# A delta-rule attention and cosine-gated feed-forward kernel: letting the build-time instruction order count TensorE's slow lengths behind pauses

## The chip, the cores and the metric

The kernel runs on one core of one Trainium2 chip. The core has five instruction queues that run side by side: TensorE (PE, matrix products), VectorE (DVE), ScalarE (ACT), GpSimd (POOL) and SyncE (SP, which here only issues transfers). Each works its instructions off in the order of the program, and waits where an instruction needs something that another queue or a transfer has yet to deliver. The metric is the device time of one execution in microseconds, median of several runs. Before the change it is 701.46 us (three runs, 700.74 to 701.78).

## The reference

The inputs are q, k, v of shape (4, 8, 768, 48), beta of shape (4, 8, 768), and two weight matrices, w_in (384, 2048) and w_out (2048, 384), all float32.

```python
# attention: delta rule, one state of 48x48 per batch and head
k_n = k / (np.linalg.norm(k, axis=-1, keepdims=True) + 1e-06)
state = np.zeros((B, H, D, D), dtype=np.float32)
for t in range(S):
    kt, vt, bt = (k_n[:, :, t], v[:, :, t], beta[:, :, t, None])
    y[:, :, t] = np.einsum('bhd,bhde->bhe', q[:, :, t], state)
    v_old = np.einsum('bhde,bhd->bhe', state, kt)
    state = state + bt[:, :, :, None] * np.einsum('bhd,bhe->bhde', kt, vt - v_old)
# bridge: (B, H, S, D) -> (B*S, H*D), then the feed-forward block
x = y.transpose(0, 2, 1, 3).reshape(B * S, H * D)      # 3072 x 384
h = x @ w_in                                           # 3072 x 2048
g = h * np.cos(h)
return g @ w_out                                       # 3072 x 384
```

The kernel works the attention off in 24 units of 32 time steps. In a unit it forms the products of keys and queries among themselves ("gram"), inverts a triangular 32x32 matrix per batch and head ("inverse", for two units at once), and then passes the state on: state product, right side, solve, update, within. The result of a unit is transposed ("features") and becomes 128 rows of x. Two units are a pair, for which the feed-forward block is computed: eight hidden products, the gate on ACT and DVE, and the output products. The units form one chain through the state; the feed-forward products fill TensorE in between.

## The kernel before

Every piece of work is a task with an engine, a cost in us, what it depends on, and a deadline. While the program is built, the class `Order` plays these tasks through with the costs given, and writes each engine's instructions in the order that results. Nothing of it runs on the chip: it settles the order in each queue and nothing else.

```python
class Order:
    WINDOW = 133.06
    LAG = {"PE": 0.2, "DVE": 0.15, "ACT": 0.15, "POOL": 0.2, "SP": 2.0}
    IN_FLIGHT = 8
    STICK = 4.36
    CHANGE = 0.15
    SMALL = ("gram", "state", "solve", "update", "within")
    BLOCK, PHASE, AHEAD, FETCH = 256, 63, 38, 3.5
    ...
    def stall(self, key, now, commit):
        # PE's instructions are counted; a block of 256 of them that is
        # fetched too late adds a wait to the task's cost
    ...
    def run(self, wrote):
        ...
                # the task with the earliest deadline that is ready and has its buffers
                if engine == "PE":
                    if (key[0] in self.SMALL) != small:
                        small = not small
                        cost += self.CHANGE
                    cost += self.stall(key, now, True)
                running[key] = item[0]
                ...
                emit()
                ...
                free[engine] = start + cost
```

The tasks that matter here, cut to their core:

```python
    # constants that the deadlines are formed with
    W_IN, W_OUT, LOADS = 62.2, 33.46, -16.83
    START = 67.36
    FIRST, STEP = 3.98, 5.5
    BASE = [START + (8 * FIRST + (p - 1) * 8 * STEP if p else 0) for p in range(NU // 2 + 2)]

    def weights(t):                 # t 0..11: pieces of w_in, 12..27: of w_out
        c = 1.0 if t < 12 else 0.8
        add(("weights", t), "SP", 0.45, lambda: narrow_load(t), ...,
            makes=[("g", ("pairs", t))], moves=1.5 * c, due=LOADS + 2 * t)
        add(("split", t), "ACT", 1.4 * c, lambda: narrow_split(t), [("weights", t)])
        add(("shift", t), "DVE", 1.4 * c, lambda: narrow_shift(t), [("split", t)])
        add(("add", t), "POOL", 1.45 * c, lambda: narrow_add(t), [("shift", t)],
            uses=[("pairs", t)], due=W_IN + 2 * t if t < 12 else W_OUT + 2 * (t - 12))

    # a unit n of the attention (m = n // 2)
        add(("turn", n), "PE", 0.9, ...)        # transposes of k and q into PSUM (p_t)
        add(("turn_out", n), "ACT", 1.25, ...)  # two copies to SBUF (kq_t)
        add(("gram", n), "PE", 0.75, ...)       # p_g
        ...
        add(("state", n), "PE", 1.3 if n else 0.0, ...)   # p_kq <- st, kq_t
        add(("right", n), "DVE", 0.58 if n else 0.0, ...) # rhs
        add(("solve", n), "PE", 0.75, lambda: solve(n), [("right", n), ("get", n)], ...)  # p_u
        add(("solve_out", n), "DVE", 1.0, ...)            # u
        add(("update", n), "PE", 0.75, ...)               # p_s; bank "two", as p_t and p_g
        add(("update_out", n), "DVE", 1.0, ...)           # st
        add(("within", n), "PE", 0.75, ...)               # p_kq <- u, tt
        add(("within_out", n), "ACT", 0.52, ...)          # y
        add(("features", n), "PE", 0.35, ...)             # p_z
        add(("features_out", n), "ACT", 0.52, ...)        # x_ffn

    # the feed-forward block of pair p; hidden(0, f) needs 3 (f // 2 % 4 + 1) pieces of w_in
            add(("hidden", *key), "PE", 2.62, lambda f=f: hidden(p, f), deps,
                makes=[("h", ("h", *key))], uses=[("x", p)],
                due=BASE[p] + f // 2 * (STEP if p else FIRST))
            add(("turns", *key), "ACT", 0.65, ...)
            add(("rest", *key), "DVE", 0.73, ...)         # r
            add(("cos", *key), "ACT", 1.45, ...)
            add(("gate", *key), "DVE", 0.73, ...)         # g_ffn
    # the first pair's output products: part k needs 4 (k + 1) pieces of w_out
```

The transfers are issued by SyncE in the written order: `load` (k, q or v of a unit, four transfers each), `narrow_load` (a piece of weights), `put` and `get` (the inverse to device memory, z_dr, and back, zt), `gram_put` and `gram_get` (g_dr and gb). The last pair's seven output products already alternate between two PSUM banks, and its first half of rows is already stored in two pieces.

Of the kernel before, what the change touches and what calls it, by code (L numbers as in the profile page):

```python
# [46 lines left out]
class Order:  # L47
# [9 lines left out]
    WINDOW = 133.06  # L57
    LAG = {"PE": 0.2, "DVE": 0.15, "ACT": 0.15, "POOL": 0.2, "SP": 2.0}
    IN_FLIGHT = 8
    STICK = 4.36  # L60
    CHANGE = 0.15
    SMALL = ("gram", "state", "solve", "update", "within")
# [8 lines left out]
    def __init__(self, bufs, free):  # L71
        self.bufs, self.free = bufs, free
        self.tasks, self.users, self.tiles = {}, {}, {}
        self.written, self.rest, self.there = 0, 0.0, {}

    def add(
# [35 lines left out]
    def run(self, wrote):  # L112
# [26 lines left out]
        count, now = len(self.tasks), 0.0  # L139
        log = []  # L140
        while events:
            now, _, key, done = heapq.heappop(events)
            if key is not None:
# [6 lines left out]
                engine, moves = self.tasks[key][0], self.tasks[key][7]  # L150
# [19 lines left out]
            for engine, heap in ready.items():  # L170
# [6 lines left out]
                if engine == "PE":  # L177
                    if (item[2][0] in self.SMALL) != small:
                        item = min(
                            (  # L180
                                x for x in able
                                if x[0] <= item[0] + self.STICK
                                and (x[2][0] in self.SMALL) == small
# [11 lines left out]
                _, cost, _, emit, _, makes, _, moves = self.tasks[key]  # L195
                if engine == "PE":
                    if (key[0] in self.SMALL) != small:
                        small = not small
                        cost += self.CHANGE
                    cost += self.stall(key, now, True)  # L200
                running[key] = item[0]
                for tag, _ in makes:
                    live[tag] += 1
# [4 lines left out]
                if moves:  # L208
                    flights = sorted(f for f in flights if f > now)
                    if len(flights) >= self.IN_FLIGHT:  # L210
                        start = flights[-self.IN_FLIGHT]
                free[engine] = start + cost
# [14 lines left out]
def kernel(  # L227
# [696 lines left out]
    )  # L924
    add = order.add
    VECTOR = {0: "one"}
    W_IN, W_OUT, LOADS = 62.2, 33.46, -16.83
    PLAIN = range(1)
    outs_done = [None]
    START = 67.36  # L930
    FIRST, STEP = 3.98, 5.5
    BASE = [START + (8 * FIRST + (p - 1) * 8 * STEP if p else 0) for p in range(NU // 2 + 2)]

# [311 lines left out]
```

## Time and profile before

| | before |
|---|---|
| time, median of 3 runs | 701.46 us |
| span of the profiled execution | 699.6 us |
| granted TensorE clock, mean | 0.997 |
| TensorE busy | 639.3 us, 91% |
| VectorE busy | 402.9 us, 58% |
| ScalarE busy | 283.2 us, 40% |
| GpSimd busy | 342.5 us, 49% |
| transfers | 49.27 MB, mean 70 GB/s |

The profile is of one execution. A line of the timeline gives the start and the length in us, the engine, the line of the kernel, the operation with the names of the tiles written and read, how many instructions are merged, and in brackets the idle time before it and what ended it. "issue" is time in which the engine waited for nothing that the profile shows. A table by stages gives each engine's busy time and number of instructions in a stretch, then the granted TensorE clock, the share of time in which the transfer engines were busy, and the rate. Names: p_t transposes, p_g gram, p_kq state product and within, p_u solve, p_s update, p_z features, p_h hidden products, p_out and p_o output products; pairs are pieces of the weights as they come from memory.

### The profile page before, as it was taken

How to read it: one execution, taken by the hardware profiler on the slowest of the kernel's cores; microseconds unless marked ns; L12 is line 12 of the kernel's file. 1: busy time of each engine (PE TensorE's matmuls, PEld its weight loads, DVE VectorE, ACT ScalarE, POOL GpSimd, SP SyncE). 2: the span in 40 equal slices, each digit the busy share in tenths (PEclk: the TensorE clock that was granted, in tenths of full speed). 3: DMA queues.
4: the chain of work that ended last, by engine and by line, in shares of the span. 5: the costliest groups of instructions: out<-in, count | busy, mean ns of one | idle time of the engine just before them, and what ended most of it. 6: DMA issues, size and time to landing. Idle time of an engine off the chain costs nothing.

```text
span 699.6 us, 25291 instructions
## 1 busy us (share of the span) xinstructions
PE 639.3 (91%) x11096; PEld 568.9 (81%) x11096; DVE 402.9 (58%) x804; ACT 283.2 (40%) x482; POOL 342.5 (49%) x738
## 2 busy tenths in 40 slices
PE   3305799999999999999999999999999999999997
PEld 2205697777898988998998988998998988988997
DVE  4895778876655545556556555556456455444542
ACT  3424467652443542532533532532532532433430
POOL 5469678878508607708607707708508508500000
PEclk9999999999999999999999999999999999999999
DMA  9888656562323133133133133132122120110000
GB/s 174 195 173 181 131 144 162 131 121 38 63 54 72 28 73 72 27 74 70 30 72 72 29 70 72 30 73 48 22 57 49 22 58 26 22 22 14 1 23 22
DMA packets 162833, 49.27 MB, mean 70 GB/s; under 512 B 154212, under 2 KB 157428, under 8 KB 162724
## 3 DMA queue, kind: packets, MB, share of 16 engines
q1 hardware_dynamic: 161252, 46.82, 32.6%
q8 instruction: 87, 1.43, 0.9%
q0 software_dynamic: 384, 0.64, 0.4%
q10 hardware_dynamic: 1088, 0.20, 0.1%
q14 instruction: 22, 0.18, 0.1%
HBM read 36.62 MB, written 11.01 MB: 68 GB/s over the span
## 4 chain that ended last, share of the span: by engine, by line
PE 86%; DMA 5%; DVE 4%; issue 1%; ACT 1%; SPq 1%; ACTq 0%; POOL 0%; DVEq 0%
PE p_h L745 32%; PE p_out L850 29%; PE p_kq L625 4%; PE p_h L728 4%; PE p_s L673 3%; PE p_kq L690 3%; PE p_out L792 3%; PE p_u L652 3%; PE p_g L514 2%; PE p_t L496 2%; PE p_o L850 1%; SPq L330 1%; DVE p_i L590 1%; DVE part_v L583 1%; DMA kp<-in_k_dram 1%
## 5 line engine op out<-in xcount | busy, mean ns | idle before, releaser
L745 PE MATMUL p_h<-x_ffn,w_in 128*128 128x256 f32 x1056 | 241.7, 381 | 1.3 <-DVE g_ffn L782 1.3
L583 POOL TENSOR_TENSOR part<-z,gb 128x126 f32<-128x126 f32 (+22 forms) x341 | 131.2, 385 | 218.4 <-DMA gb<-g_dr 167.0
L745 PEld LDWEIGHTS p_h<-x_ffn,w_in 128*128 128x128 f32 x1056 | 197.1, 190 | 26.8 <-PE p_kq L625 1.0
L590 POOL TENSOR_TENSOR z<-z,part 128x126 f32<-128x126 f32 (+22 forms) x341 | 137.1, 402 | 26.7
L762 DVE SCALAR_TENSOR_TENSOR r<-p_h,turns 128x512 f32<-128x512 f32 x96 | 66.1, 689 | 114.9 <-ACT turns L758 113.7
L850 PE MATMUL p_out<-w_out,g_ffn 128*128 128x192 f32 x672 | 126.0, 333 | 0.8
L758 ACT ACTIVATE turns<-p_h 128x512 int32<-128x512 f32 x96 | 57.1, 594 | 167.6 <-PE p_h L745 154.2
L850 PEld LDWEIGHTS p_out<-w_out,g_ffn 128*128 128x128 f32 x672 | 108.7, 190 | 6.2 <-ACT o L887 3.0
L782 DVE TENSOR_TENSOR g_ffn<-r,p_h 128x512 f32<-128x512 f32 x96 | 65.5, 683 | 53.0 <-ACT r L770 52.7
L850 PE MATMUL p_out<-w_sum,g_ffn 128*128 128x192 f32 x496 | 89.7, 329 | 0.2 <-DVE o L900 0.2
L866 DVE TENSOR_TENSOR g_ffn<-g_ffn 128x256 f32<-128x256 f32 x176 | 79.2, 471 | 15.0 <-PE p_out L850 13.0
L769 ACT ACTIVATE r<-r 128x512 f32<-128x512 f32 x96 | 60.7, 632 | 62.0 <-DVE r L762 61.9
L850 PEld LDWEIGHTS p_out<-w_sum,g_ffn 128*128 128x128 f32 x496 | 81.7, 190 | 2.3 <-DVE o L900 0.4
L770 ACT ACTIVATE r<-r,halfpi 128x512 f32<-128x512 f32 x96 | 69.3, 722 | 3.1
L496 PE MATMUL p_t<-consts,kp 128*128 128x128 f32 x96 | 16.8, 305 | 41.2 <-DMA vp<-in_v_dram 29.6
L900 DVE SCALAR_TENSOR_TENSOR o<-p_out,o 128x192 f32<-128x192 f32 x74 | 25.4, 356 | 48.5 <-PE p_out L850 48.2
L496 PEld LDWEIGHTS p_t<-consts,kp 128*128 128x128 f32 x96 | 13.0, 157 | 43.8 <-issue 38.1
L701 ACT COPY y<-p_kq 128x384 f32<-128x384 f32 x24 | 11.5, 479 | 69.5 <-PE p_kq L690 69.5
L455 POOL TENSOR_TENSOR knrm<-ksum,halves 128x16 f32<-128x16 f32 (+1 forms) x14 | 36.5, 2613 | 5.9 <-DVE ksum L443 3.3
L625 PEld LDWEIGHTS p_kq<-st,kq_t 48*32 48x32 f32 x2944 | 29.4, 107 | 7.1 <-issue 7.0
L625 PE MATMUL p_kq<-st,kq_t 48*32 48x48 f32 x2944 | 32.8, 216 | 1.6 <-issue 1.6
L502 ACT COPY kq_t<-p_t 128x512 f32<-128x512 f32 x48 | 25.7, 588 | 15.9 <-PE p_t L496 15.9
(73 smaller groups left out, 619.8 us busy)
## 6 DMA issues: line engine op xcount, KB each, us to landing
pairs<-in_moe_w_in_dram SPq DMA_DIRECT2D x12, 512.0 KB
gb<-g_dr SPq DMA_DIRECT2D x24, 256.0 KB
pairs<-in_moe_w_out_dram SPq DMA_DIRECT2D x16, 384.0 KB
vp<-in_v_dram SPq DMA_DIRECT2D x96, 48.0 KB
kp<-in_k_dram SPq DMA_DIRECT2D x92, 48.0 KB
qp<-in_q_dram SPq DMA_DIRECT2D x92, 48.0 KB
out_dram<-o SPq DMA_DIRECT2D x23, 192.0 KB
g_dr<-g SPq DMA_DIRECT2D x24, 128.0 KB
```

The costliest lines, as they stand in the source:

```text
L496: nc.tensor.transpose(p_t[:, a, j], src[:, 2 * j : 2 * j + 2], ident)
L583: eng.tensor_tensor(out=part, in0=z[:, 0:rows, j, None].to_broadcast(shape), in1=a[:, j, None, j + 1 :].to_broadcast(shape), op=ALU.mult,)
L590: eng.tensor_tensor(out=behind, in0=behind, in1=part, op=ALU.subtract)
L625: nc.tensor.matmul(p_kq[quarter(b), par, a, j], kq_t[rows48(par), a, j, quarter(b)], st[rows48(par), b // 2, j, b % 2], start=(j == 0 and ...
L745: nc.tensor.matmul(p_h[:, i], w_in[:, t, (f + i) * 128 : (f + i + 1) * 128], xts[p][:, t], start=(t == 0), stop=(t == KT - 1),)
L758: nc.scalar.activation(turns[p, f], p_hs[p, f], AF.Copy, scale=TURN)
L762: nc.vector.scalar_tensor_tensor(out=r, in0=p_hs[p, f], scalar=TURN, in1=turns.pop((p, f)), op0=ALU.mult, op1=ALU.subtract,)
L769: nc.scalar.activation(r, r, AF.Abs)
L770: nc.scalar.activation(r, r, AF.Sin, bias=halfpi, scale=-2.0 * math.pi)
L782: nc.vector.tensor_tensor(out=out, in0=rests.pop((p, f)), in1=p_hs.pop((p, f)), op=ALU.mult,)
L850: nc.tensor.matmul(p_o, left(p, e // 2, a)[:, e % 2], right(e, b), start=(e == 0), stop=(e == FT // 2 - 1), skip_group_check=True,)
L866: nc.vector.tensor_tensor(out=left(p, k, to), in0=left(p, k, one), in1=left(p, k, two), op=op)
```

## The change

The build-time order now holds that TensorE is slow behind pauses. It keeps the moment at which TensorE's latest stretch of work began. A gap of more than 0.6 us starts a new stretch, a gap of more than 2.0 us makes the engine cold, 5.0 us of a stretch make it warm again, and the cost of a task on the cold engine counts twice. With it go three constants of the deadlines: those for w_out's addition and for the loads of weights lie later, by 10.3 and 3 us, and so do those for the feed-forward products, by 2.64 us. The kernel's arithmetic and its instructions are the same; what the change is for is an order of them that suits the engine's real lengths at the start.

```diff
@@ class Order
     IN_FLIGHT = 8
+    WARMING = 5.0
     STICK = 4.36
@@ __init__
         self.tasks, self.users, self.tiles = {}, {}, {}
+        self.since, self.last, self.cold = 0.0, 0.0, True
         self.written, self.rest, self.there = 0, 0.0, {}
@@ run
                     cost += self.stall(key, now, True)
+                if engine == "PE" and cost:
+
+                    if now - self.last > 0.6:
+                        self.since = now
+                    if now - self.last > 2.0:
+                        self.cold = True
+                    if now - self.since > self.WARMING:
+                        self.cold = False
+                    cost *= 2.0 if self.cold else 1.0
+                    self.last = now + cost
                 running[key] = item[0]
@@ tile_deltanet__then__act_gcu_kernel
-    W_IN, W_OUT, LOADS = 62.2, 33.46, -16.83
+    W_IN, W_OUT, LOADS = 62.2, 43.76, -13.83
     PLAIN = range(1)
     outs_done = [None]
-    START = 67.36
+    START = 70
```

## The prediction

> **What bounds the kernel now.** I read the slices of the page first, then the busy times by stage, then the waits of TensorE (PE), then the engines' lines in order of time around each wait.
>
> The slices: 40 of 17.5 us each, in tenths busy; PEclk is the granted clock.
> ```profile
> PE   3305799999999999999999999999999999999997
> PEclk9999999999999999999999999999999999999999
> ```
> PE is full from the sixth slice on, and a program of fixed matmuls can't be made shorter there. Only the first five slices and the last are open.
>
> The same by stage (us; busy time of each engine and count of instructions, then clock, DMA share, GB/s):
> ```profile
> 0.00:55.15 55.15, 12.41 (x288) 10.13 (x289) 39.80 (x123) 19.37 (x34) 30.75 (x52) 1.00 0.86 176
> 55.15:115.00 59.85, 50.06 (x1349) 45.74 (x1350) 41.73 (x68) 33.40 (x61) 47.48 (x76) 0.97 0.70 168
> 115.00:200.00 85.00, 83.56 (x1362) 67.21 (x1365) 61.25 (x111) 42.69 (x75) 59.41 (x111) 1.00 0.41 82
> 200.00:694.90 494.90, 493.28 (x8122) 445.78 (x8108) 259.80 (x502) 187.79 (x313) 204.88 (x501) 1.00 0.23 45
> 694.90:699.60 4.70, 0.00 (x0) 0.00 (x0) 0.36 (x1) 0.00 (x0) 0.00 (x0) 0.97 0.17 58
> ```
> PE idles 42.7 us before 55.15 (loads, then the first inverse on VectorE, DVE, from 29.4 to 47.5), 9.8 us in 55 to 115, 1.4 in 115 to 200, 1.6 in the next 495, 4.7 behind the last matmul. So what a new order can win after 55 us is under 13 us of idle time, plus matmuls slowed by the cold clock.
>
> PE's waits from 55 to 200 us (us in total, times, longest):
> ```profile
> PE p_u L652 <- issue: 1.8, 1, 1.8
> PE p_h L728 <- issue: 1.7, 1, 1.7
> PE p_s L673 <- ACT kq_t L502: 1.6, 1, 1.6
> PE p_kq L625 <- issue: 1.6, 1, 1.6
> PE p_s L673 <- DVE u L660: 1.4, 1, 1.4
> PE p_h L745 <- DVE g_ffn L782: 1.3, 2, 0.9
> PE p_h L728 <- DVE r L762: 0.7, 1, 0.7
> ```
> They are many and short, each with another cause. The third is an update (L673) placed right behind a transpose whose result ScalarE (ACT) must still copy out of the same PSUM bank. Two "issue" waits fall where the build-time order's own bookkeeping puts a fetch of PE instructions behind many short matmuls (a state product is 128 of them in 1.4 us).
>
> PE in order of time, the cold clock (start, us, instructions):
> ```profile
> 71.13 4.18 PE L728 MATMUL p_h<-x_ffn,w_in 128*128 128x128 f32 x21 [1.67 <-issue]
> 77.20 2.94 PE L728 MATMUL p_h<-x_ffn,w_in 128*128 128x128 f32 x24
> 88.04 1.25 PE L625 MATMUL p_kq<-st,kq_t 48*32 48x48 f32 x89 [1.56 <-issue]
> 89.22 4.14 PE L728 MATMUL p_h<-x_ffn,w_in 128*128 128x128 f32 x24
> ```
> The same 24 matmuls take 2.94 us or 4.14 us. PE warms by 75.2, and is slow once more from 88 to 93.
>
> [...] the relapse at 88 follows pauses of 1.65, 0.26 and 1.56 us only. The change's rule (cold behind a pause over 2.0 us) wouldn't see this relapse, but would see the one after the long wait. The slow copy is 1.4 times as long here, not 2.
> [...] k, q and v come in rows of 192 B; the page counts 154212 of 162833 packets under 512 B, and the DMA share is 0.86 in the first stage at 176 GB/s. So the order of DMA issues early on matters.
> [...] the weights' shift on DVE (L417) takes 0.68 us at 78.1 and 1.58 us at 86.2, where POOL works too.
>
> **The change part by part.** No instruction is added or removed: PE has the same 5680 matmuls as the program counts them, and its last 495 of 602 groups stand in the same order, as do the last 60 rows of the other queues. PE goes over from small to large matmuls and back 160 times before, 158 after. The constants are only deadlines of the build-time order. So the gain is the difference in the moment at which PE reaches the common order, near 160 us; behind it I expect nothing.
>
> Up to the first state product PE's order is equal. Two things come earlier or later before it. The SyncE queue now:
> ```profile
> 48.17 0.39 SPq L599 DMA_DIRECT2D z_dr<-z  x1
> 48.61 4.88 SPq L330 DMA_DIRECT2D vp<-in_v_dram  x4
> 53.53 0.45 SPq L403 DMA_DIRECT2D pairs<-in_moe_w_in_dram  x1
> 54.08 4.81 SPq L608 DMA_DIRECT2D zt<-z_dr  x8
> ```
> Behind the store of the inverse come one v load, one piece of weights, then the inverse's reload (zt), for which the first solve waits at 58.93. After: the weights, a whole k load, the v load, then zt. Four more issues at 0.48 us (v's 1.9 us per four elsewhere) are **+1.9 us** for the first solve. Behind it, now, DVE does u only at 61.23, 0.3 us after the solve, for a weights shift; after, that shift stands before, so **-0.3**. But ACT's copy of y then stands behind the split of w_in's next to last piece, and x_ffn behind a square that needs a k load: I allow **+0.6**. The first hidden product so starts 2.2 us later; its fetch wait (1.67) stays.
>
> Then the order differs. Now: hidden, solve, gram, hidden, transpose, update, within, gram, features, state, hidden. After: hidden twice, gram, solve, transpose, hidden, update, within, features, hidden, gram, one output product, hidden twice, state. In this:
> - a hidden product lies between transpose and update: **-1.65**, ACT's two copies (1.07) hide under its 2.9 us;
> - gram no longer follows the state's sum directly: **-0.26**;
> - state comes behind six hidden products instead of two, so its instructions are fetched under long matmuls: **-1.56**;
> - without these pauses, no relapse of the clock: 4.14 - 2.94 = 1.2, and 0.3 on the 89 matmuls (0.96 at the warm 1.38 per 128): **-1.5**;
> - the third hidden product needs nine pieces of w_in, which POOL adds behind the second inverse (end 77.0). POOL now waits 4.35 us in its queue:
> ```profile
> 82.59 1.02 POOL L426 TENSOR_TENSOR w_out<-w_out,pairs 128x384 uint32<-128x384 uint32 x1 [4.35 <-DVE w_out L422]
> 83.56 3.79 POOL L426 TENSOR_TENSOR w_in<-w_in,pairs 128x512 uint32<-128x512 uint32 x3
> ```
> After, w_out's first pieces are issued by SyncE before the stores of the second inverse and fourth gram, not behind them, so this wait should vanish: one w_out, one w_in, one w_out, two w_in are 1.0 + 1.3 + 1.0 + 2.6 = 5.9 us, until 82.9. PE arrives at about 82.1 (76.3 end of the first, + 2.9 + 0.8 + 0.9 + 1.2): **+0.8**.
> Sum: +1.9 - 0.3 + 0.6 - 1.65 - 0.26 - 1.56 - 1.5 + 0.8 = **-2.0 us**. In 100 to 160 the waits of 0.7 (r) and 1.3 (g_ffn) stem from DVE queued behind w_out pieces; after, w_out is nearly done earlier, three pieces before the third inverse. But the output products want them earlier too: the third product at about 118 against 133 now, with POOL's twelfth piece at 115 to 117. Half of the 2.0 us saved: **-1.0**. That is 3.0 less in all; rounding for what I can't see in the queues, I take 2.7: **698.8 us**.
>
> **Rivals.** *The start decides against it.* If zt, y and x_ffn together cost 4 to 5 us instead of 2.2, the gain is eaten: 701 to 702. For it: DMA is the busy part there (share 0.86), and ACT takes pieces in order. Against it: a k load moves out of the stretch behind.
> *The output products wait for w_out.* POOL interleaves these adds with the third inverse; if gb comes 3 us late, each of two products waits some 2 us: 702 to 704. For it: PE now has that gram 7 us later. Against: SyncE now blocks gb until 92.4 though it is ready earlier.
> *The new order avoids nearly all waits.* All idle time of 62 to 130 (about 7 us) and the relapse gone, and zt not late: 695. For it: this is what the cold clock in the build-time order is for. Against: the order's idea of DMA times was not changed.
> *Nothing moves*, as PE is full from 90 us on: within 1 us of 701.5. Against it: idle time before 90 shifts everything behind.
>
> **Range and chances.** The terms sized from single rows add up to -5.0 and +3.3; the start is uncertain by some 2 us and the output products by 2. Range 695.4 to 702.4. A 2% step is 14 us, more than all idle time behind 55 us, so faster by over 2% 0.02, within 0.96, slower 0.02.
>
> **What would show it.** In the changed kernel: the first solve at about 60.5 instead of 58.9; no wait of update on kq_t; no issue wait at a state product near 86; hidden products of 2.9 us throughout from 77 on; a wait of under 1 us of the third hidden product on POOL; busy time of PE some 1.5 to 2 us less; all behind 200 us shifted as a block. I'm wrong if PE's waits on w_in or w_out pieces exceed 3 us, if the first solve moves by over 3 us, or if the stretch behind 200 us changes length.

## The result

| | before | after |
|---|---|---|
| time, median of 4 runs each, same comparison | 701.28 us (700.74 to 701.78) | 707.68 us (706.85 to 708.43) |
| ratio to before | | 1.0091, 95% interval 1.0074 to 1.0109 |
| span of the profiled execution | 699.6 us | 705.1 us |
| TensorE busy | 639.3 us | 639.7 us |

The prediction was 698.8 us, with a range up to 702.4. The kernel became 6.4 us slower instead of 2.7 us faster, and the time lies outside the range.

The profile after, first its slices (tenths busy, then the granted clock):

```profile
PE   3306887999999999999999999999999999999997
...
PEclk9755899999999999999999999999999999999999
```

The sixth and the seventh slice (88 to 123 us) have fallen from 9 tenths to 8 and 7, the fifth has risen from 7 to 8; from the eighth on PE is full as before. The stages that answer to those shown of before (us; busy time and instructions of PE, PE's weight loads, DVE, ACT, POOL; clock, DMA share, GB/s):

```profile
0.00:55.15 55.15, 12.52 (x291) 10.49 (x292) 40.10 (x123) 19.90 (x36) 30.52 (x52) 0.75 0.88 188
55.15:115.00 59.85, 45.16 (x999) 40.02 (x1000) 40.22 (x66) 31.19 (x59) 46.53 (x71) 0.80 0.73 171
115.00:200.00 85.00, 82.77 (x1575) 66.80 (x1565) 57.55 (x106) 39.73 (x71) 59.49 (x116) 1.00 0.35 68
200.00:600.00 400.00, 399.15 (x7203) 358.60 (x7199) 217.50 (x414) 158.54 (x265) 195.57 (x475) 1.00 0.27 53
```

PE has 45.16 us of work in the second stage where it had 50.06, and 82.77 in the third where it had 83.56. Behind 200 us it is as full as it was. So the loss is made between 55 and about 160 us. PE's waits over the whole execution (us in total, times, longest):

```profile
...
PE p_u L664 <- issue: 4.3, 1, 4.3
PE p_z L719 <- ACT y L713: 3.4, 2, 2.4
...
PE p_h L740 <- issue: 1.7, 1, 1.7
PE p_kq L637 <- issue: 1.4, 2, 1.2
PE p_h L740 <- DVE g_ffn L794: 1.4, 1, 1.4
PE p_s L685 <- DVE u L672: 1.4, 2, 1.1
...
PE p_h L740 <- POOL w_in L438: 1.0, 2, 0.8
```

One wait stands out, and it is one that before didn't have: 4.3 us inside a solve, "issue", that is, PE had nothing to wait for that the profile shows. Waits of this kind are called fetch waits below; that PE waits in them for its own instructions is shown further on. In order of time around it (start, us, instructions, idle before):

```profile
102.42 1.38 PE L637 MATMUL p_kq<-st,kq_t 48*32 48x48 f32 x128
103.73 0.66 PE L508 MATMUL p_t<-consts,kp 128*128 128x128 f32 x4
...
104.76 0.78 PE L664 MATMUL p_u<-rhs,zt 32*32 32x48 f32 x52
109.88 0.53 PE L664 MATMUL p_u<-rhs,zt 32*32 32x48 f32 x12 [4.34 <-issue]
110.34 4.18 PE L740 MATMUL p_h<-x_ffn,w_in 128*128 128x128 f32 x24
```

State of unit 2, transpose of unit 6 and 52 of the 64 matmuls of the solve of unit 2 run without a gap; then PE stands still for 4.34 us, and the 24 matmuls of the hidden product behind take 4.18 us, where they take 2.94 us at a granted clock of 1.00 (before, at 77.2 us). To see what is chance, both kernels were profiled twice (the second records are of runs told below). "Stretch" is the time from the transpose of unit 4 to the solve of unit 4, which both orders have; "fetch" is the sum of the "issue" waits in it, without the one ahead of the first solve, which I count with the waits for zt; "rest" is what follows the stretch. All in us of the record:

| record | transpose 4 at | stretch | PE busy in it | fetch | other idle | rest | span |
|---|---|---|---|---|---|---|---|
| before | 55.1 | 103.7 | 92.7 | 3.2 | 7.8 | 540.7 | 699.6 |
| before, second | 53.6 | 102.1 | 91.3 | 3.8 | 7.0 | 539.5 | 695.3 |
| after | 54.5 | 109.3 | 92.8 | 7.2 | 9.3 | 541.3 | 705.1 |
| after, second | 54.9 | 109.3 | 94.2 | 7.2 | 7.8 | 541.7 | 705.9 |

The stretch is 6.4 us longer (109.3 against a mean of 102.9): 3.7 us of it are fetch, 1.1 other idle time, 1.6 PE's own work at a lower clock. Within the other idle time the waits for y grew by 2.5 us (3.44 and 2.84 us in the stretch against 0.60 twice), and the 1.65 us of before for kq_t are gone. After also still owes one transpose at its end (about 1.0 us, in the rest), so the low clock weighs some 2.5 us. Fetch and the stretch repeat from record to record; how the remainder divides between waits for data and low clock does not. The mean clock of the record (0.963 after, 0.997 in the first record of before) is no trace of the change: the second record of before has 0.965.

### The profile page after: what moved, and what is told of

It reads as the page before. It is cut to its first block, busy times and chain, and to the rows that moved or that the text cites. A ratio compares the mean times of both kernels' runs of the same rounds, so it can differ in the third digit from the quotient of the medians.

```text
span 705.1 us, 25290 instructions
## 1 busy us (share of the span) xinstructions
PE 639.7 (91%) x11096; PEld 568.5 (81%) x11096; DVE 401.6 (57%) x804; ACT 282.6 (40%) x482; POOL 341.6 (48%) x738
## 3 DMA queue, kind: packets, MB, share of 16 engines
q8 instruction: 87, 1.43, 0.9%
## 4 chain that ended last, share of the span: by engine, by line
PE 84%; DMA 5%; POOL 4%; issue 2%; DVE 2%; SPq 1%; ACT 1%; DVEq 0%; POOLq 0%
PE p_h L757 33%; PE p_out L862 28%; PE p_kq L637 4%; PE p_u L664 3%; PE p_out L804 3%; PE p_kq L702 3%; PE p_s L685 2%; PE p_t L508 2%; PE p_h L740 2%; PE p_g L526 2%; DMA kp<-in_k_dram 2%; POOL z L602 2%; POOL part L595 2%; PE p_o L862 1%; DMA pairs<-in_moe_w_in_dram 1%
## 5 line engine op out<-in xcount | busy, mean ns | idle before, releaser
L862 PEld LDWEIGHTS p_out<-w_out,g_ffn 128*128 128x128 f32 x672 | 108.7, 190 | 6.2 <-ACT o L899 3.0
```

The source lines that it names most:

```text
L862: nc.tensor.matmul(p_o, left(p, e // 2, a)[:, e % 2], right(e, b), start=(e == 0), stop=(e == FT // 2 - 1), skip_group_check=True,)
```

## The experiments

Six comparisons were made, each with its own runs of before; their medians of before lie between 697.6 and 701.3 us, so only ratios to before within a comparison are set side by side.

### One half of the change at a time

The rule of the cold clock with the old constants (rule_only):

```diff
-    W_IN, W_OUT, LOADS = 62.2, 43.76, -13.83
+    W_IN, W_OUT, LOADS = 62.2, 33.46, -16.83
-    START = 70
+    START = 67.36
```

> The cold-clock rule with the old constants. If the rule alone makes the loss: about 1.009 of before (707 to 708 us). If the constants make it: about 1.000. Theory A (fetches of PE instructions that fall behind short matmuls): counted in blocks of 128 matmuls from the fetch wait in the first hidden product, one block edge falls on matmul 120 of the second state product, with 147 matmuls of only some 2 us ahead of it, so an issue wait of 3 to 5 us there; 703 to 706 us in all. Theory B (ScalarE's queue, copies of y behind pieces of weights): waits of features on y of over 2 us as in the changed kernel and little else.

The three new constants without the rule (const_only; the edit is made to before):

```diff
-    W_IN, W_OUT, LOADS = 62.2, 33.46, -16.83
+    W_IN, W_OUT, LOADS = 62.2, 43.76, -13.83
-    START = 67.36
+    START = 70
```

> The three constants without the rule. If the constants make the loss: 707 us. If the rule makes it: 701. Theory A: a block edge on matmul 104 of the second state product, an issue wait of 2 to 4 us there; 702 to 705 us. Theory B: waits on y above 2 us only if the y copy stands behind the weights here too.

Measured: rule alone 1.0078 (1.0053 to 1.0103), constants alone 1.0102 (1.0070 to 1.0135), against 1.0091 for both. Neither half is the good one. Each makes its own order. In the state of unit 2 PE waits ahead of the 119th matmul for the rule (the 120th was expected) and of the 104th for the constants (as expected), but for less time: 2.33 us where 3 to 5 were expected, and 0.26 where 2 to 4 were. The constants have their long fetch waits elsewhere, 3.83 us at the first hidden product, 1.92 in a gram and 0.80 in the state of unit 4; those of the stretch add up to 6.8 us, and the stretch takes 108.0 us. The rule has only 2.8 us of fetch in its stretch of 104.1 us, less than before has. Its longest wait is for y, and so for the rule alone the fetch does not explain the loss. Both waits of the rule in the timeline:

```profile
67.94 0.90 PE L719 MATMUL p_z<-consts,y 128*128 128x128 f32 x3 [4.52 <-ACT y L713]
...
91.83 1.28 PE L637 MATMUL p_kq<-st,kq_t 48*32 48x48 f32 x116
95.44 0.30 PE L637 MATMUL p_kq<-st,kq_t 48*32 48x48 f32 x10 [2.33 <-issue]
95.67 4.54 PE L740 MATMUL p_h<-x_ffn,w_in 128*128 128x128 f32 x24
```

The second looks like the case above: a pause of 2.33 us in the midst of one group, then a hidden product of 4.54 us.

### Where PE waits for its own instructions

The page has two queues of instructions, one of 87 packets and one of 22. By its size the first is PE's:

```profile
q8 instruction: 87, 1.43, 0.9%
```

1.43 MB in 87 packets are 16.4 KB each. PE's 2 times 11096 matmuls and weight loads are 22192 instructions, 255 for each of the 87 packets. The long "issue" waits bear it out: in after, the fourth matmul of the first hidden product, the 53rd of the solve of unit 2 and the 101st of the state of unit 4 lie 636 and 638 matmuls apart, about 5 times 127.3; 128 matmuls with their weight loads are 256 instructions, and by my estimate 0.5% of other instructions in the queue would make it 127.3. From 102 to 109 us after's record has a single packet on this queue, and it is counted between 107 and 108 us, while PE stands still in the solve (105.5 to 109.9 us). So edges of blocks can be counted out on PE's list, and a fetch wait should lie at one. (Not every "issue" wait is one: in the run of the y copy below, 1.21 us of "issue" stand ahead of the transposes at 82.25 us, 46 matmuls behind an edge.) As a theory: a block is asked for 147 matmuls ahead of its edge (256 and 38 instructions, which the build-time order assumes in its bookkeeping). Ahead of the wait in the solve of unit 2 these are 2.7 us of work, from 102.8 to 105.5 us; 147 matmuls of hidden products at 2.94 us for 24 would be 18 us.

Then 92 additional matmuls (46 small products in the gram of unit 3, where PE waits anyway) move every later edge without moving anything else in the list:

```diff
+        if n == 3:
+            idle = bank("h", [128, 4, 128], "p_idle")
+            for _ in range(46):
+                nc.tensor.matmul(
+                    idle[quarter(0), 0, 0 : 2 * C],
+                    kq_t[rows48(0), 0, 0, quarter(0)],
+                    kq_t[rows48(0), :, 0, quarter(0)],
+                )
```

Nothing reads their result. Once in after, once in before:

> The changed kernel with 46 small products (92 matmuls) more in TensorE's long pause at 27 to 54 us, written to a bank that nobody reads; the order of all else is unchanged. Theory A: all block edges move 92 matmuls ahead. The wait of 4.34 us inside the third solve (matmul 52) vanishes from there and comes back as some 2.5 us at the end of the hidden product behind it (matmul 24); the wait of 1.68 us at matmul 3 of the first hidden product vanishes, as the edge now lies in the second hidden product. 3 to 4 us less than the changed kernel: 703.5 to 704.5 us. Theory B and any theory of data or transfers: the waits stay where they are, and the time stays at 707 to 708.

> The same 92 matmuls in the kernel before. Theory A: the wait of 1.67 us in the first hidden product vanishes (the edge moves to matmul 15 of the second solve), the one in the second state product moves from matmul 39 to 75 and grows from 1.56 to some 2.2 us: about 1 us less, 700 us. Theory B: no change, 701.3.

And 64 products, 256 instructions, which leave the edges where they were:

> The kernel after with 64 small products (128 matmuls with as many weight loads, so 256 instructions) more in the gram of unit 3, unread, where the earlier run had 46. 256 instructions leave every later block edge where it lies in after, 184 moved it. Theory of the 256 instruction blocks: the waits are at the places of after again, 3 to 4.5 us in the solve of unit 2, the state of unit 4 at its 100th product, none of the fetch waits of 1.8 and 2.4 us at 310 and 471 us that 46 products brought, and the time is 1.007 to 1.013 of before, not 1.023. Rival (46 products cost 6 us because work was added): ratio 1.02 or more.

Measured: after with 46 products 1.0232 (1.0193 to 1.0272), before with 46 products 1.0236 (1.0209 to 1.0264), after with 64 products 1.0154 (1.0118 to 1.0190; after itself had 1.0124, 1.0094 to 1.0153, in the comparison ahead of it). The edges obeyed: with 46 products in after neither the wait in the solve of unit 2 nor the one at the first hidden product is there; in before the wait in the state of unit 2 moved from its 40th to its 76th matmul and grew from 1.56 to 2.26 us. But my expectation of a gain was wrong by 10 us and more. In the stretch of after with 46 products the fetch waits fell to 4.5 us (2.39 us now in a gram, 1.39 at an output product), and yet it takes 111.8 us, as other idle time is 12.8 us. And I had counted the edges only up to 130 us. In the steady part the new phase puts edges into the state products, over and over. After with 46 products:

```profile
307.71 1.09 PE L645 MATMUL p_kq<-st,kq_t 48*32 48x48 f32 x96
310.62 0.40 PE L645 MATMUL p_kq<-st,kq_t 48*32 48x48 f32 x30 [1.82 <-issue]
```

A second such wait, 2.37 us, comes at 471.46, again at the 99th matmul. With them the rest of the execution is 548.4 us against 541.3 (before with 46: 549.6 against 540.7). With 64 products the rest is 540.5, the waits at 310 and 471 us are gone, and the one in the solve is back at its 53rd matmul:

```profile
106.36 0.78 PE L672 MATMUL p_u<-rhs,zt 32*32 32x48 f32 x52
110.34 0.52 PE L672 MATMUL p_u<-rhs,zt 32*32 32x48 f32 x12 [3.20 <-issue]
110.79 4.37 PE L748 MATMUL p_h<-x_ffn,w_in 128*128 128x128 f32 x24
```

So the added work itself costs little and the phase of the blocks decides: the block of 256 instructions is shown. (1.0154 lies above the 1.007 to 1.013 that I expected, but its interval overlaps with that of after.) It also suggests that the steady order is tuned to this phase.

### Why the block in the solve took so long

From the state's 41st matmul, where the theory has the block asked for (about 102.8 us), to 109.9 us are 7.1 us. In the two records of before the same reckoning gives 4.3 and 3.5 us for the wait in the state of unit 2. In after the loads of k and q of units 8 and 9 and pieces of w_out move in just that time, so they were put behind the last pieces of w_out; PE's list stays as it is:

```diff
+        for keys, ahead in (
+            ((("k", 8), ("k", 9), ("q", 8), ("q", 9)), ("k", 10)),
+            ((("square", 4, 0), ("sum", 4, 0)), ("norms", 4, 0)),
+        ):
+            moved = [x for key in keys for x in lines if x[0] == key]
+            lines = [x for x in lines if x[0] not in keys]
+            at = [x[0] for x in lines].index(ahead)
+            lines[at:at] = moved
```

("lines" is the list of tasks in the order that the class found; here it is rearranged ahead of being written.) It took three forms, which differ in where the squares, sum, norms and scale of unit 8 went:

> The kernel after with TensorE's list untouched: the loads of k and q of units 8 and 9, which move at 99 to 112 us in rows of 192 bytes and are needed only at about 180 us, go behind the last pieces of w_out and the load of v of unit 7; the squares, sum, norms and scale of unit 8 go behind them. If the fetch of the block in the solve of unit 2 took its 7 us because it queued behind these transfers: the wait of 4.34 us in that solve shrinks to 1 to 2 us, the hidden product behind it needs no cold clock (4.18 to about 2.9 us), and the time falls by 2.5 to 4.5 us against after. If the fetch's length has nothing to do with the load on the DMA engines, or if the pieces of w_out alone hold it up: the wait stays above 3.5 us and the time within 1 us of after.

> The kernel after, TensorE's list untouched, with the loads of k and q of units 8 and 9 behind the last pieces of w_out, and only the squares and the sum of unit 8 moved behind them; the norms and the scale stay where they were, so that VectorE no longer stands 9 us behind them, as it did in the first form of this run. Theory that the fetch queues behind the transfers of data: the wait in the solve of unit 2 is 2 to 2.5 us again instead of 4.34 us, with little else changed: 1.5 to 2.5 us faster than after, ratio 1.0055 to 1.007. Rival (chance in one record): wait above 3.5 us, ratio 1.009.

> The kernel after with the loads of k and q of units 8 and 9 behind the last pieces of w_out, and now the squares and the sum of unit 8 just ahead of their norms (about 165 us), so that neither ScalarE nor VectorE stands behind these loads, as both did in the first two forms. In the second form TensorE reached the first 256 wide hidden product at 131.6 us, where after reached it at about 135 us, and lost it again to a wait of 4.61 us for g_ffn, behind the squares on ScalarE. Theory that the fetch queues behind the transfers of data: the wait in the solve of unit 2 is 2 to 2.5 us, that wait for g_ffn is gone, and the time is 2.5 to 4 us under after in the same comparison: ratio to before 1.0035 to 1.0055. Rival (some other wait takes the time back, or there was no gain): within 1 us of after.

Measured: 1.0260 (1.0240 to 1.0280), 1.0187 (1.0152 to 1.0222) and 1.0161 (1.0131 to 1.0191), the last with after at 1.0124 beside it: all slower. The local effect came all the same, three times out of three. The stages around the wait, first after's second record, then the second form (columns as above; the last but one is the DMA share):

```profile
102.00:108.00 6.00, 3.27 (x190) 2.78 (x190) 3.77 (x6) 5.08 (x10) 4.02 (x10) 1.00 1.11 292
```
```profile
103.00:108.00 5.00, 3.48 (x192) 2.99 (x192) 3.37 (x7) 4.18 (x8) 3.09 (x9) 1.00 0.70 260
```

| records | DMA share while the block was awaited | wait in the solve of unit 2 |
|---|---|---|
| k and q loads in place (after, after second, 64 products, y copy below) | 0.99, 1.11, 1.12, 1.14 | 4.34, 3.27, 3.20, 3.75 us |
| k and q loads later (three forms) | 0.73, 0.70, 0.66 | 2.35, 1.95, 2.48 us |

The shares are those from the 41st matmul of the state to the end of the wait; they add up the times of packets, so they can exceed 1. The loads account for 1.4 us of a mean wait of 3.6 us. The share by itself does not give the length: at 1.03 and 0.94 the waits of before come from fetches of 4.3 and 3.5 us by this reckoning, and with the constants alone a fetch takes 3.5 us at a share of 0.08 (125.3 to 128.8 us). In the second form PE reached the first 256 wide hidden product at 131.6 us, 3.2 us ahead of after, and lost it here:

```profile
145.40 2.75 PE L767 MATMUL p_h<-x_ffn,w_in 128*128 128x256 f32 x12
152.76 5.41 PE L767 MATMUL p_h<-x_ffn,w_in 128*128 128x256 f32 x12 [4.61 <-DVE g_ffn L804]
158.01 1.45 PE L814 MATMUL p_out<-w_out,g_ffn 128*128 128x384 f32 x4
```

4.61 us for the gate, which stood on ScalarE behind the moved squares, whose k had not landed; and the hidden product behind is cold, 5.41 us for 12 matmuls that take 2.75. In the third form these squares were out of the way, but the next ones were not. ScalarE in that record:

```profile
152.93 0.84 ACT L460 ACTIVATE ksq<-kp 128x768 f32<-128x768 f32 x1 [4.12 <-POOL z L612]
153.68 0.58 ACT L780 ACTIVATE turns<-p_h 128x512 int32<-128x512 f32 x1
```

The sixteen issues of the four moved loads keep SyncE busy from 134.1 to 144.6 us, so k of unit 11 is issued at 149.3 instead of 137.5 us (after, second record), and its squares hold ScalarE for 4.12 us (the record names POOL's inverse as what ended the wait; k of unit 11, issued until 151.1, fits as well). The gate behind comes late, and PE waits 3.08 us for it. With the low clock of that record (5.46 us for the product at 91.98, 5.49 for the one at 112.56) this is more than the gain. So: that these loads lengthen this fetch is shown; that moving them helps, in these places, is refuted.

The same loads moved in the rule-alone kernel, where they run behind its fetch wait:

> The rule alone with the old constants, and the loads of k of unit 9 and q of units 8 and 9 behind the last pieces of w_out, the squares, sum, norms and scale of unit 8 at about 160 to 170 us. The fetch wait of 2.33 us in the state of unit 2 of the rule alone lies at 93 to 95 us, ahead of these loads (about 106 to 115 us), so by the theory of queueing it stays; time within 1.5 us of the rule alone (ratio 1.0078 to its before, 1.006 to 1.010 here). If it falls to a ratio under 1.004, these loads cost something other than the fetch.

1.0088 (1.0056 to 1.0121), with a wait of 2.9 us in the state of unit 2: nothing gained, as the theory had it.

### The wait for y

On ScalarE the copy of y of unit 0 is put ahead of the pieces of weights, and the square that stood before the copy of x_ffn goes behind it (the lines that carry this out are left out):

```diff
+        for key, ahead in ((("within_out", 0), ("split", 10)), (("square", 3, 0), ("sum", 3, 0))):
```

> The kernel after with two copies moved on ScalarE and nothing else: the copy of y of unit 0 ahead of the pieces of weights it stood behind, and the copy of x_ffn of unit 0 ahead of the squares of the keys. Theory of ScalarE's queue (the 2.37 us wait of the features for y is part of the loss): the wait shrinks to under 1 us, state, hidden products and all that follows come some 1.6 us earlier, and the time falls by 1.6 us against after. Fetch theory: the first hidden product reaches its third matmul 1.6 us earlier, but the fetch of that block lands when it did (about 71.7 us), so the wait there grows from 1.68 to about 3.3 us and the time stays within 0.5 us of after.

1.0114 (1.0094 to 1.0134), where after had 1.0091 and 1.0124: the time stayed. The wait for y fell from 2.37 to 0.60 us as meant. The fetch wait behind it did not grow to 3.3 us, though; it is 1.40 us. In this record everything up to the first solve came 2 us later than in after (59.22 against 57.15), more than the copy saves, and a start that scatters by 2 us between records can't tell 1.6 us. That the fetch swallowed the gain is therefore not shown; that taking away this wait alone does not bring the time back is.

### Orders that count on a longer fetch

The build-time order reckons with 3.5 us for a fetch. Counting on 5.5 us, it puts a hidden product between the transpose and the solve of unit 2 and an output product behind the solve:

```diff
-    BLOCK, PHASE, AHEAD, FETCH = 256, 63, 38, 3.5
+    BLOCK, PHASE, AHEAD, FETCH = 256, 63, 38, 5.5
```

> The kernel after with one number changed: the build-time order counts on 5.5 us for the fetch of the next 256 TensorE instructions (before and after: 3.5). Up to the transpose of unit 6 TensorE's list is that of after. Then a hidden product (0.12) stands between that transpose and the solve of unit 2, and an output product between that solve and the update. The block edge lies in the same solve, 24 products earlier in it, and the fetch has some 5.0 instead of 2.4 us of named work ahead of it. Fetch theory: the 4.34 us wait in the solve of unit 2 shrinks to 1.5 to 2.0 us or less, the hidden product behind it runs at full clock (2.9 instead of 4.18 us), and the time falls by 2.5 to 4.5 us against after (707.7), so to 703.2 to 705.2 on the scale of the first comparison. Rival (the loss is that of a data wait or of the transfers, the fetch only shows it): the wait turns up again at the same time under another name and the time stays within 1 us of after.

> The kernel before with the same one number, 5.5 us for 3.5. The block edges with the shortest work ahead of them (hidden product f 0, 2.2 us, and the state of unit 2, 2.2 us) stay where they are, so the two fetch waits of 1.67 and 1.56 us stay; edges later in the start get 4 to 10 us of work. Fetch theory: no data wait of the start changes by design, so the time is within 1.5 us of before, with the sign set by what the new order does to the data waits. Rival (a longer fetch time is simply better for any order): 2 us faster than before or more.

Measured: 1.0205 (1.0185 to 1.0224) for after and 1.0136 (1.0118 to 1.0154) for before, both worse. The wait itself behaved as expected:

```profile
108.95 0.53 PE L664 MATMUL p_u<-rhs,zt 32*32 32x48 f32 x28
110.14 0.61 PE L664 MATMUL p_u<-rhs,zt 32*32 32x48 f32 x36 [0.66 <-issue]
110.69 2.85 PE L804 MATMUL p_out<-w_out,g_ffn 128*128 128x384 f32 x8
```

0.66 us instead of 4.34. But the number rules the whole program: the rest became 548.1 us (541.3), in before 546.5 (540.7). So the number was changed only up to the first 3300 instructions, for after and for the rule alone:

```diff
-                there[(i + self.PHASE + self.AHEAD) // self.BLOCK + 1] = t + self.FETCH
+                there[(i + self.PHASE + self.AHEAD) // self.BLOCK + 1] = t + (5.5 if self.written < 3300 else self.FETCH)
```

> The kernel after, with the build-time order counting on 5.5 us for a fetch only up to the first 3300 TensorE instructions it writes (about 160 us) and on 3.5 us from there as before. TensorE's tasks differ from those of after in nine moves, all before about 160 us and one swap of a state and a solve later; the steady part keeps its order, which the earlier run with 5.5 us throughout did not. Fetch theory: as in that run the wait in the solve of unit 2 is under 1 us instead of 4.34 us and the hidden product behind it runs at full clock; nothing is given back later, so the time is 2.5 to 4 us under after: ratio to before 1.0035 to 1.006, where after has 1.009. Rival (the gain of the fetch is given back by data waits in the same stretch, as the run with 5.5 us throughout suggested): ratio 1.008 or more.

> The rule alone with the old three constants, with the same local 5.5 us. Against the run of the rule alone (ratio 1.0078) the block edge that fell 1.6 us behind its request in the state of unit 2 (wait 2.33 us, then a hidden product at the low clock, 4.54 us) gets a hidden product ahead of it; a later edge in the solve of unit 4 has only 2.3 us ahead. Fetch theory: the 2.33 us wait and the 1.6 us of low clock go, one of 1 to 2 us comes at that solve: 1.5 to 3 us faster than the rule alone, ratio 1.0035 to 1.0055. Rival (data waits take the place): ratio 1.007 or more.

Measured: 1.0088 (1.0052 to 1.0123) and 1.0101 (1.0063 to 1.0139). The rest is 540.9 us again. The fetch waits of the stretch fell from 7.2 to 4.2 us in after, that in the solve of unit 2 to 0.99 us. And the stretch became only 0.6 us shorter (108.7 against 109.3): the rival won. What came instead, one unit later:

```profile
125.75 0.88 PE L664 MATMUL p_u<-rhs,zt 32*32 32x48 f32 x64
129.16 1.36 PE L685 MATMUL p_s<-u,kp 64*64 64x96 f32 x32 [2.53 <-DVE u L672]
130.46 1.50 PE L702 MATMUL p_kq<-u,tt 32*32 32x48 f32 x64
```

The update of unit 3 waits 2.53 us for u, because the gram and the output product that lay between its solve and it in after now stand ahead of the solve, and PE then runs at the low clock again (1.36 and 1.50 us for what takes 0.89 and 0.88).

### Everything at once

The local 5.5 us, the y copy and the moved loads, in two forms (the squares as in the second and in the third form above):

> The kernel after with three things at once: the local 5.5 us for a fetch, the loads of k and q of units 8 and 9 (with their squares and sum) behind the pieces of w_out, and the copy of y of unit 0 ahead of the pieces of weights on ScalarE. If these name the whole loss against before: no fetch wait above 1.5 us after the first hidden product, the y wait under 1 us, and the time within 2 us of before (ratio 0.998 to 1.003). If the start itself still owes 2 us (the low clock, the wait for g_ffn of 1.4 us, fetches at other places): ratio 1.003 to 1.006.

> The local 5.5 us for a fetch, the copy of y of unit 0 ahead of the pieces of weights on ScalarE, and the loads of k and q moved as in the run beside it. The first form of these three together reached the first 256 wide hidden product at 131.3 us and lost 3.91 us at 141.9 us to ScalarE, which stood behind the squares; that wait should go. If fetch, its queueing behind transfers and the y copy make up the loss: 4 to 6 us under after in the same comparison, ratio to before 0.999 to 1.004. Rival: within 2 us of after.

1.0152 (1.0117 to 1.0186) and 1.0131 (1.0099 to 1.0163). Fetch waits in the stretch are down to 2.3 and 1.9 us, less than before has, and yet the stretch is 111.1 and 111.0 us: other idle time is 16.1 and 13.8 us. The causes named do not add up as if each could be taken away by itself. But the moved loads are in both forms, and alone they had made the stretch longer (112.5 and 115.0 us in their second and third form, 119.7 in the first). The local 5.5 us together with the y copy, without these loads, was not run; in the run of the local 5.5 us alone the waits for y are still 3.5 us.

### Both kernels once more

> The kernel after once more, as the reference of this comparison: TensorE's list and every other engine's are those of after. Expected by every theory: ratio to before 1.007 to 1.011, a fetch wait of 3.5 to 4.5 us in the solve of unit 2 and a wait of about 1.4 us at g_ffn.

> The kernel before once more, against itself, for a second record of it: ratio 0.997 to 1.003. From its first record: fetch waits of 1.67 and 1.56 us at the first hidden product and in the state of unit 2, no low clock between 75 and 160 us, and the solve of unit 4 some 104 us after the transpose of unit 4. If the waits at other engines or the low clock scatter between two records of one order as they do between the two of after (109.3 us each, but 9.1 and 7.7 us of waits for data, and 92.8 and 94.2 us busy), the sum of the two is what can be compared and not each.

After: 1.0124 (1.0094 to 1.0153), a little above what I gave; before against itself 1.0002 (0.9987 to 1.0017). The second record of before has its fetch waits where they must be (start, us, instructions):

```profile
83.75 0.59 PE L627 MATMUL p_kq<-st,kq_t 48*32 48x48 f32 x39
85.11 1.03 PE L627 MATMUL p_kq<-st,kq_t 48*32 48x48 f32 x89 [0.78 <-issue]
...
98.01 0.74 PE L516 MATMUL p_g<-kq_t 48*32 48x64 f32 x51
99.96 0.34 PE L516 MATMUL p_g<-kq_t 48*32 48x64 f32 x13 [1.20 <-issue]
```

Again inside the state of unit 2 behind its 39th matmul, 0.78 us this time, and one of 1.20 us at the edge in a gram 380 matmuls (three blocks) on, where the first record had none. So the places are fixed by the list, and the lengths scatter by about a microsecond.

## Why the prediction was wrong

By its own steps:

- *"Four more issues ... are +1.9 us for the first solve."* It didn't come. From the transpose of unit 4 to the start of the first solve are 2.7 us in both records of after and 3.8 and 3.7 in those of before, but after's solve then waits inside for pieces of zt, 0.2 to 0.8 us each. Before, then after:

```profile
58.93 2.00 PE L652 MATMUL p_u<-vp,zt 32*32 32x48 f32 x64 [1.84 <-issue]
```
```profile
57.15 0.33 PE L664 MATMUL p_u<-vp,zt 32*32 32x48 f32 x2 [0.71 <-DMA zt<-z_dr]
57.79 0.51 PE L664 MATMUL p_u<-vp,zt 32*32 32x48 f32 x4 [0.31 <-DMA zt<-z_dr]
58.61 1.48 PE L664 MATMUL p_u<-vp,zt 32*32 32x48 f32 x58 [0.31 <-DMA zt<-z_dr]
```

  The solve ends 5.6 and 6.2 us behind the start of the transpose, against 5.8 and 5.7: +0.1 in the mean.
- *"-0.3"* for u: the wait was 1.39 and 1.18 us and is 1.14 twice, so about half of it.
- *"+0.6"* for y and x_ffn: the place was right, the size not. PE waits 2.37 and 2.24 us for y where it waited 0.60 us: +1.7, and once more behind the next within (1.07 and 0.60 us): +2.5 in all. The run with the copies moved took the wait away and left the time as it was.
- *"-1.65"* and *"-0.26"*: both came true; neither wait is left.
- *"state comes behind six hidden products instead of two, so its instructions are fetched under long matmuls: -1.56."* This is the step that failed. The wait did leave the state. But I checked the one edge that before's wait lay at, not the next: 128 matmuls on, 200 short matmuls (state, transpose, solve) in 3 us, by the theory asked for in the midst of them. There PE waits 4.34 and 3.27 us, and 1.18 and 1.48 us more in the state of unit 4. The fetch waits of the stretch rose from 3.5 to 7.2 us (means): +3.7 for a predicted -1.56. The 1.56 us were also partly chance: in the second record of before this wait is 0.78 us.
- *"without these pauses, no relapse of the clock: -1.5."* It fell with the step ahead of it: the pause in the solve is itself followed by the low clock, 4.18 and 4.57 us for 24 matmuls of 2.9. PE's own work in the stretch became longer by 2.5 us (with the transpose that after still owes) instead of shorter by 1.5. In the second record of before there was no such relapse to win back: behind the 0.78 us the 24 matmuls take 2.94 us.
- *"+0.8"* for the third hidden product at w_in: 1.03 us in one record of after, nothing in the other. The +0.8 also came of a slip: the first hidden product's end was taken as 76.3 us, but the 75.3 of before and the 2.2 us of delay make 77.5, and from there PE would have come at 83.3 us, behind the piece.
- *"-1.0"* for later waits: those at 112, 131 and 140 us (0.71, 0.90, 0.37) did go, 2.0 us; a new one for g_ffn at 90 us is 1.40 and 1.26 us.

Under the range, the gains sized from single rows add up to 5.3 us and not 5.0, as the 0.3 for u was left out.

What I took for certain, "all behind 200 us shifted as a block", held: the rest is 1.4 us longer in the mean, about 1.0 of it the transpose still owed. Of the rivals, "the output products wait for w_out" (702 to 704) came nearest to the time, but PE waits for no piece of w_out in either record of after. "The start decides against it" (701 to 702) had y in it rightly, but zt, which it also named, cost 0.1 us.

How far this is shown. That the wait in the solve is a fetch at a block edge is shown by its place in every record and by the moved edges. That it is made longer by the loads of k and q beside it is shown too. That it is *the* cause of the loss, in the sense that without it the kernel would be as fast as before, is refuted by the run that took it down to 1 us and gained 0.6 us of the stretch. Of the 6.4 us of the stretch the fetch waits are the largest part in the sum, 3.7 us, and behind them there seems to stand a second limit: the chain of solve, u, update and state of units 2 to 4 with too few long products left to lie between. Both orders have the same products; after uses hidden products in two blocks of two ahead of it (45 matmuls at 71.8 us, 48 at 97.0), where before deals them out singly. That this is the reason is argued from the two timelines, not tested: no run rearranged the products over the whole stretch. Nor is it explained why the rule alone, whose record has a stretch of 104.1 us and a span of 699.2, was timed 0.78% above before; its before has no record of the same comparison, and the record is of the fastest of its four executions (701.03 of 701.03 to 703.91 us). What keeps after slower once the wait in the solve is gone therefore stays open. No version found beats before.

## What to carry to other kernels

Where an engine runs hundreds of tiny instructions in a row, count its list in the blocks in which instructions are loaded (256 on PE here), and check every edge of the new order, not only those at which the old one waited; a change of a few instructions anywhere ahead shifts all edges behind. A wait taken out of a chain that is close to its limit elsewhere is worth what the next wait leaves of it: find by a run with that wait gone, before adding it to a sum. And profile both kernels twice before a difference of a microsecond is given a cause.

## What was unexpected of the hardware

- PE's instructions come in packets of 16.4 KB (87 packets, 1.43 MB), 256 at a time by the places of the waits. Reckoned from 147 matmuls ahead of an edge, the point that the build-time order assumes, a block took from 3.4 us (after with 46 products, the edge at 310 us) to 7.1 us (after, in the solve). At the first hidden product the same reckoning gives 6.3 us in both records of before and 8.1 and 8.3 in those of after, so where a block is asked for is not settled; in the steady part, at a DMA share of 0.3, an edge with 1.6 us of work ahead still cost 1.8 and 2.4 us.
- Behind which pauses the clock fell back, the change's limit of 2.0 us does not tell. 24 matmuls of 2.9 us took 4.54 us behind a pause of 2.33 us, and 4.55 us behind one of 1.41 us in one record (5.5 us for a fetch throughout), while behind a pause of 1.40 us in after they took 2.92 us. A pause of 1.95 us in the second form of the moved loads had no such effect: the 24 matmuls behind it took 2.94 us.
- In before and in after the clock's changes lie on a grid of their own: the times between two changes, from 20 to 600 us, are 4 and 1 times 3.41 us in before (changes at 74.68, 88.33, 91.75) and 14, 10 and 1 times in after (27.63, 75.41, 109.55, 112.96). Windows of this grid in before and in after, and one of the same length in the second form of the moved loads (columns as above; PE's busy time comes first, the clock is third from the end):

```profile
84.92:88.33 3.41, 1.85 (x132) 1.45 (x110) 2.77 (x5) 1.40 (x3) 2.64 (x3) 1.00 0.88 183
88.33:91.75 3.42, 3.42 (x89) 3.30 (x69) 2.43 (x3) 1.51 (x3) 3.42 (x3) 0.50 0.64 158
```
```profile
89.07:92.48 3.41, 2.01 (x18) 1.85 (x17) 3.18 (x6) 1.33 (x4) 2.65 (x3) 1.00 0.41 64
106.14:109.55 3.41, 0.00 (x0) 0.00 (x0) 1.13 (x3) 1.93 (x4) 1.97 (x5) 1.00 0.92 200
109.55:112.96 3.41, 3.08 (x24) 2.96 (x24) 2.52 (x4) 0.00 (x0) 1.79 (x5) 0.50 0.64 174
```
```profile
106.79:110.20 3.41, 1.77 (x25) 1.71 (x25) 2.84 (x6) 2.22 (x5) 2.10 (x4) 1.00 0.48 143
```

  PE is idle for 1.56 us in the first and for all of the fourth, and the clock falls at their ends; behind 1.40 us in the third and 1.64 us in the last it stays. In the windows of before and after that are not shown, from 78 to 200 us, the clock is at 1.00 and PE's idle time at most 1.42 us (before, 81.51 to 84.92), and it stays behind each of them. So 1.56 us of idle time came ahead of a fall and 1.64 us did not, and one limit on the single pause, as the change sets it, cannot tell these cases apart. Whether the place of a pause on this grid decides is not shown.
- The first stage's clock is not fully recorded. Before has 1.00 for 0 to 55 us and 0.73 in its second record, but the first four matmuls of the transposes of unit 4 take 1.08 us in both and 0.60 us once PE is warm, so the clock was low at 55 us in both. The mean clock of a record therefore says nothing about a change here.
